# Retention attention and a PReLU block on one core: the first batch's two large parts in chunks of 128 tokens instead of 64, and three unread products ahead of the first unit instead of two

## The chip, the cores and the metric

The kernel runs on one core of one Trainium2 chip. The metric is the device time of one execution in microseconds, and lower is better. The time before is the median of 9 runs. A profile was taken of one more execution; every duration below comes from it.

## What is computed

The reference is a retention layer (attention without a softmax, with a decay for the distance between tokens) over 8 batches, 8 heads, 576 tokens and 64 columns a head, followed by a two-layer block over all 8 x 576 = 4608 tokens. All of it is in float32.

```
scores = (q @ k.T) / sqrt(64)                     # per batch and head, 576 x 576
gamma  = 1 - 2 ** (-5 - h)                        # h = 0..7
D      = gamma ** (i - j) if i >= j else 0
x      = (scores * D) @ v                         # to (4608 tokens, 512)
h      = x @ w_in                                 # 512 -> 2048
g      = max(h, 0) + alpha * min(h, 0)
out    = g @ w_out                                # 2048 -> 512
```

The decay splits into a factor for the query's place and one for the key's, so a sequence can be taken in chunks: inside a chunk the masked scores are multiplied by v; what earlier chunks give is a 64 x 64 state k.T @ v for each head, the running sum of the earlier chunks' products, multiplied by q.

## The kernel before

**Two phases on TensorE.** The two-layer block works on blocks of 256 tokens (`kb`, 18 of them) and on 8 slices of the 2048 columns (`i`). One pair (kb, i) is a unit. The units of blocks 0 and 1 are plain: `plain_unit` (line 419) makes 8 products of 128x128 by 128x256 into `ph` (L426), ACT makes the two halves of the activation (L430, L432), DVE joins them (L442), and `mlp_out`/`plain_out` (line 397) makes 4 products of 128x512 into `po` (L405). All later units go through a scheme of 7 products for 8 (L470, L388), for which GpSimd first combines the weights. The weights come in 32 pieces of 512 KB by DMA. Each piece is rewritten on its way: two ACT instructions (L296, L298, `piece_in`), three on DVE (L307, L310, L312) and one sum on GpSimd (L314, `piece_out`). Pieces 0 and 1 hold the first layer's weights of unit slice 0, pieces 2 and 3 the second layer's; pieces 4 to 7 do the same for slice 1, and so on.

**The first batch.** While the weights are on their way, the first batch's attention is done by functions of its own, and its token blocks are the plain ones. Its 576 tokens are cut into three parts (`PARTS`): two large ones of 256 tokens, x = 0 and x = 1, and a last one of 64. All eight heads of a part are done together, two heads to a pair (`c`, four pairs), one head on array rows or columns 0 to 63, the other on 64 to 127. For a large part these steps follow each other:

- `part_scale` (L675): GpSimd multiplies q and v by their factors.
- `part_transposes` (L695): TensorE turns k and q, ACT copies them to kT and qT (L702), DVE the last one of part 0 (L700).
- `part_scores` (L714): 32 products, each of one chunk of 64 tokens for one head, in four quarters of the array. In part 0 DVE multiplies by the mask (L721), in part 1 ACT copies (L723) and GpSimd multiplies (L724).
- `part_states` (L734): 32 products k.T @ v, one for each chunk of 64 and each head, then running sums over the four chunks: in part 0 by ACT copies and GpSimd sums (L742, L744), in part 1 by DVE (L746).
- `part_carry` (L750): GpSimd scales the last sum for the next part.
- `part_values`: 32 products of the masked scores with v (L762); then for each chunk that has a state before it (three in part 0, four in part 1) 16 products of 32 columns of the state with qT (L773), so 48 and 64. ACT copies the result into `xb` (L779, L781).

**The order.** Each engine takes its instructions in the order of the text at lines 823 to 890; there the parts' steps, the pieces and the first units are laid one after another by hand. After part 0's values TensorE makes two products of 128x512 that nothing reads (L842, "idle"), the transpose of alpha (L845), and the first plain unit (0, 0). Part 1's transposes stand around that unit's `mlp_out`, then come its scores and states, unit (0, 1), its values, the last part's transposes (L789), and the output products of (0, 1). The last part's scores are L798; later pairs of heads in the second phase go through L559, L577, L616 and L652.

**Buffers.** PSUM banks come from `ps_a` (two banks that rotate), `ps_h` and `ps_o` (by name: `pso0` to `pso3`). In part 0 kT, qT and the masked scores are tiles "g" of the pool `mlp`, which has three buffers in rotation; the units' own g tiles take the same three. In part 1 they lie in parts of `w_out` that are still unused.

A float32 product shows as two instructions on TensorE in the trace, each with its own weight load; a transpose shows as one. The lines around the unread products:

```
    idle = ps_h.tile([P, DM], FP32, tag="psh0", name="idle")
    for _ in range(2):
        nc.tensor.matmul(idle, ident, part[0][0][:, 0].rearrange("p h d -> p (h d)"),
                         start=True, stop=True)
```

Of the kernel before, what the change touches and what calls it, by code (L numbers as in the profile page):

```python
# [10 lines left out]
FP32 = mybir.dt.float32  # L11
# [7 lines left out]
def kernel(  # L19
# [121 lines left out]
    def room(i, s0, n):  # L141
# [5 lines left out]
        "p (m h d) -> p m h d", h=H, d=D) for i in (2, 3, 4)] for x in range(2)]  # L147
    part.append([room(i, 4, 2).rearrange("p (m h d) -> p m h d", h=H, d=D) for i in (2, 3, 4)])
    sums = [[room(i, s0, 1).rearrange("p (c d) -> p c d", d=D) for i, s0 in x] for x in (
        ((5, 4), (5, 5), (5, 6), (6, 4)), ((6, 5), (6, 6), (7, 4), (7, 5)), ())]  # L150
    carry = [None] + [room(i, 6, 1).rearrange("p (c d) -> p c d", d=D) for i in (2, 7)]

    def load_part(x):
# [26 lines left out]
    zero = const.tile([P, D], FP32, name="zero")  # L180
    nc.gpsimd.memset(zero, 0.0)

    mask = const.tile([P, C], FP32, name="mask")
    nc.gpsimd.memset(mask, 1.0)
    for p2 in range(2):
        nc.gpsimd.affine_select(out=mask[p2 * C:(p2 + 1) * C], in_=mask[p2 * C:(p2 + 1) * C],
                                compare_op=ALU.is_ge, fill=0.0, base=0, pattern=[[1, C]],
                                channel_multiplier=-1)

    dif = const.tile([P, NBIT, H], FP32, name="dif")  # L190
    for h in range(H):
# [358 lines left out]
    def pair_scores(n, kT, qT):  # L550
        c = pairs[n][1]

        mt = attn.tile([P, 2 * S], FP32, tag="at", name=f"mt_{n}").rearrange(
            "p (h j s) -> p h j s", h=2, s=C)
        ps = [ps_tile([P, NM, C], f"ps{p2}_{n}") for p2 in range(2)]
        for j in range(NJ):
            for h2 in range(2):
                x = (1 - h2, h2)[j % 2]
                nc.tensor.matmul(ps[j % 2][half(x), j // 2], kT[half(h2), chunk(j)],  # L559
                                 qT[half(h2), chunk(j)], start=True, stop=True)  # L560
        for h2 in range(2):
            nc.scalar.copy(mt[half(h2), h2].rearrange("p j s -> p (j s)"), qT[half(h2)])
        for p2 in range(2):
            for h2 in range(2):
                h, to, x = 2 * c + h2, half(1 - h2), (1 - h2, h2)[p2]
                nm = NM - p2
                nc.vector.scalar_tensor_tensor(
                    out=mt[to, h2, p2::2], in0=ps[p2][half(x), 0:nm], scalar=th[to, 3, h:h + 1],
                    in1=mask[to, None, :].to_broadcast([C, nm, C]), op0=ALU.mult, op1=ALU.mult)
        return mt  # L570

    def pair_states(n, kn, vn):
# [33 lines left out]
    def pair_front(n, kT, qT, kn, vn, extra):  # L606
# [20 lines left out]
        for h2 in range(2):  # L627
            to = half(1 - h2)
            nc.vector.scalar_tensor_tensor(  # L629
                out=mt[to, h2, NJ - 1], in0=extra[to],  # L630
                scalar=th[to, 3, 2 * c + h2:2 * c + h2 + 1], in1=mask[to],
                op0=ALU.mult, op1=ALU.mult)
        for p2 in range(2):
            for h2 in range(2):
                h, to, x = 2 * c + h2, half(1 - h2), (1 - h2, h2)[p2]
                nc.vector.scalar_tensor_tensor(  # L636
                    out=mt[to, h2, p2:NJ - 1:2], in0=ps[p2][half(x), 0],
                    scalar=th[to, 3, h:h + 1],
                    in1=mask[to, None, :].to_broadcast([C, NM - 1, C]),
                    op0=ALU.mult, op1=ALU.mult)  # L640
        later.append(lambda: pair_sums(vn, running_sums(n, ps[0][:, 1], ps[1][:, 1])))

# [44 lines left out]
    def part_transposes(x, i):  # L687
# [5 lines left out]
        for m in range(2):  # L693
# [7 lines left out]
            else:  # L701
                nc.scalar.copy(to, fro)  # L702

    def part_scores(x):
        at = tat[x] = (mlp.tile([P, 8 * P], FP32, tag="g", name=f"pa_{x}") if x == 0 else
                       room(4, 0, 4)).rearrange("p (h n) -> p h n", h=2)
        banks = part_banks(x, 2 if x == 0 else None, "ps")
        kT, qT = tT[x, 0], tT[x, 1]
        for m in range(2):
            for c in range(NPAIR):  # L710
                for p2 in range(2):
                    for h2 in range(2):
                        j = chunk(2 * m + p2)
                        nc.tensor.matmul(banks[h2][half(p2), (2 * c + m) * C:(2 * c + m + 1) * C],  # L714
                                         kT[half(h2), c, j], qT[half(h2), c, j],
                                         start=True, stop=True)
        for h2 in range(2):
            to, fro = [t.rearrange("p (n s) -> p n s", s=C) for t in (at[:, h2], banks[h2])]
            m = mask[:, None, :].to_broadcast([P, 8, C])
            if x == 0:  # L720
                nc.vector.tensor_tensor(out=to, in0=fro, in1=m, op=ALU.mult)  # L721
            else:
                nc.scalar.copy(to, fro)  # L723
                nc.gpsimd.tensor_tensor(out=to, in0=to, in1=m, op=ALU.mult)  # L724

    def part_states(x):
        kn, vn = part[x][0], part[x][2]
        banks = [t.rearrange("p (m c d) -> p m c d", m=2, c=NPAIR)
                 for t in part_banks(x, None if x == 0 else 0, "pu")]
        for m in range(2):  # L730
            for c in range(NPAIR):
                for p2 in range(2):
                    for h2 in range(2):
                        nc.tensor.matmul(banks[p2][half(h2), m, c], kn[half(p2), m, 2 * c + h2],  # L734
                                         vn[half(p2), m, 2 * c + h2],
                                         start=(m == 0 and c == 0),
                                         stop=(m == 1 and c == NPAIR - 1), skip_group_check=True)
        was = carry[x]
        for j in range(4):
            u = banks[j % 2][:, j // 2]  # L740
            if x == 0:
                nc.scalar.copy(sums[x][j], u)  # L742
                if j:
                    nc.gpsimd.tensor_tensor(out=sums[x][j], in0=was, in1=sums[x][j], op=ALU.add)  # L744
            else:
                nc.vector.tensor_tensor(out=sums[x][j], in0=was, in1=u, op=ALU.add)  # L746
            was = sums[x][j]

    def part_carry(x):
        nc.gpsimd.tensor_tensor(out=carry[x + 1], in0=sums[x][3],  # L750
                                in1=gch[:, 2, :, None].to_broadcast([P, NPAIR, D]), op=ALU.mult)

    def part_values(x):
        vn, qT, at = part[x][2], tT[x, 1], tat[x]
        banks = [t.rearrange("p (c m s) -> p c m s", c=NPAIR, m=2)
                 for t in part_banks(x, 0 if x == 0 else None, "pv")]
        for m in range(2):
            for c in range(NPAIR):
                for p2 in range(2):
                    for h2 in range(2):  # L760
                        n = 2 * c + m
                        nc.tensor.matmul(banks[p2][half(h2 ^ p2), c, m],  # L762
                                         vn[half(p2), m, 2 * c + h2],
                                         at[half(p2), h2, n * C:(n + 1) * C],
                                         start=(m == 0 and c == 0), stop=False,
                                         skip_group_check=True)
        for j in range(1 if x == 0 else 0, 4):
            su = sums[x][j - 1] if j else carry[x]
            for c in range(NPAIR):
                for h2 in range(2):  # L770
                    for e in range(0, D, 32):
                        to = (h2 ^ (j % 2)) * D + e
                        nc.tensor.matmul(banks[j % 2][to:to + 32, c, j // 2],  # L773
                                         su[half(h2), c, e:e + 32], qT[half(h2), c, chunk(j)],
                                         start=False, stop=(j >= 2), skip_group_check=True)
        xb[x] = ring.tile([P, NCC, TB], FP32, tag=f"x{x}", name=f"xb_{x}")
        to = xb[x].rearrange("p c (m q s) -> p q c m s", m=2, q=2)
        for c in (slice(0, 2), slice(2, 4)) if x == 0 else (slice(0, NPAIR),):
            nc.scalar.copy(to[:, 0, c], banks[0][:, c])  # L779
            for h2 in range(2):  # L780
                nc.scalar.copy(to[half(h2), 1, c], banks[1][half(1 - h2), c])  # L781


    def last_transposes():
# [8 lines left out]
    def last_scores():  # L793
# [5 lines left out]
                                 start=True, stop=True)  # L799
        for h2 in range(2):  # L800
            nc.vector.tensor_tensor(out=at[0:C, h2], in0=ps[h2][0:C],
                                    in1=mask[0:C, None, :].to_broadcast([C, NPAIR, C]),
                                    op=ALU.mult)

    def last_values():
# [23 lines left out]
    part_transposes(0, 0)  # L829
    part_transposes(0, 1)  # L830
    part_scale(0, 2)
    part_scores(0)
    piece_in(1)
    part_states(0)
    piece_in(2)
# [2 lines left out]
    part_values(0)  # L838

    idle = ps_h.tile([P, DM], FP32, tag="psh0", name="idle")  # L840
    for _ in range(2):
        nc.tensor.matmul(idle, ident, part[0][0][:, 0].rearrange("p h d -> p (h d)"),  # L842
                         start=True, stop=True)
    aps = ps_a.tile([P, NFC], FP32, tag="psa", name="aps")
# [13 lines left out]
    mlp_out(lambda: part_transposes(1, 1))  # L858
    piece_out(1)
    piece_in(1)  # L860
    part_scores(1)
    piece_out(1)
    part_states(1)
    piece_in(1)
# [167 lines left out]
```

## Time and profile before

| what | value |
|---|---|
| median of 9 runs | 1011.19 us (1009.38 to 1014.33) |
| the profiled execution | 1012.03 us, its span 1010.3 us |
| TensorE busy (PE) | 995.0 us, 98% of the span |
| VectorE busy (DVE) | 772.7 us, 76% |
| ScalarE busy (ACT) | 267.4 us, 26% |
| GpSimd busy (POOL) | 179.0 us, 18% |
| first product of L695, L714, L734, L762, L773 in part 0 | 5.15, 10.38, 12.14, 13.58, 14.92 us |
| first unread product (L842), first product of unit (0, 0) | 18.26, 20.40 us |
| first product of part 1's scores, of unit (0, 1), of part 1's values | 30.35, 34.58, 38.23 us |

The span runs from the first to the last recorded instruction of the core. PE is TensorE's products and PEld its weight loads, SP the engine that issues most DMAs. "L714" is line 714 of the kernel. In the chain that ended last, each piece shows its start, its duration and what ran, followed back from the last instruction through whatever released it; "issue" is time in which the profile shows nothing that the engine waited for. A window's row shows the window, its length, and for each engine the busy time and, in brackets, how many instructions were in flight in it, then the granted clock, the DMA share and GB/s. A share of busy time is a mean over the whole span; what a step in the first 50 us costs is read from windows and the timeline there.

### The profile page before, as it was taken

How to read it: one execution, taken by the hardware profiler on the slowest of the kernel's cores; microseconds unless marked ns; L12 is line 12 of the kernel's file. 1: busy time of each engine (PE TensorE's matmuls, PEld its weight loads, DVE VectorE, ACT ScalarE, POOL GpSimd, SP SyncE). 2: the span in 40 equal slices, each digit the busy share in tenths (PEclk: the TensorE clock that was granted, in tenths of full speed). 3: DMA queues.
4: the chain of work that ended last, by engine and by line, in shares of the span. 5: the costliest groups of instructions: out<-in, count | busy, mean ns of one | idle time of the engine just before them, and what ended most of it. 6: DMA issues, size and time to landing. Idle time of an engine off the chain costs nothing.

```text
span 1010.3 us, 23133 instructions
## 1 busy us (share of the span) xinstructions
PE 995.0 (98%) x9389; PEld 891.9 (88%) x9389; DVE 772.7 (76%) x2086; ACT 267.4 (26%) x605; POOL 179.0 (18%) x201
## 2 busy tenths in 40 slices
PE   6899999999999999999999999999999999999998
PEld 5666668999999999999999999999999999999997
DVE  7669967887878878686777788878778776666665
ACT  5556663222222222022122222222222210000000
POOL 5656674310100020100010000200010001010000
PEclk9999999999999999999999999999999999999999
DMA  9985745232322312131121122323222000000000
GB/s 229 245 201 140 185 73 120 49 72 48 69 48 49 68 37 63 18 69 31 40 48 48 36 56 48 69 48 69 48 43 52 13 22 1 22 1 22 1 22 22
DMA packets 229595, 64.30 MB, mean 64 GB/s; under 512 B 214368, under 2 KB 223088, under 8 KB 229488
## 3 DMA queue, kind: packets, MB, share of 16 engines
q1 hardware_dynamic: 227088, 62.02, 27.4%
q8 instruction: 74, 1.21, 0.5%
q10 hardware_dynamic: 2400, 0.79, 0.4%
q14 instruction: 33, 0.27, 0.1%
HBM read 53.35 MB, written 9.44 MB: 62 GB/s over the span
## 4 chain that ended last, share of the span: by engine, by line
PE 98%; DMA 1%; issue 0%; DVE 0%; ACT 0%; SPq 0%; DVEq 0%
PE ph L470 40%; PE po L388 38%; PE ph L426 6%; PE po L405 6%; PE pv L652 3%; PE ps L616 1%; PE ps L622 1%; DMA w_out<-in_k_dram 1%; PE pv L966 1%; PE pt L695 0%; PE ps L714 0%; PE ps L559 0%; PE pv L773 0%; PE pu L734 0%; PE pu L577 0%
## 5 line engine op out<-in xcount | busy, mean ns | idle before, releaser
L388 PE MATMUL po<-w_out,g 128*128 128x256 f32 x1792 | 408.2, 379 | 0.0
L388 PEld LDWEIGHTS po<-w_out,g 128*128 128x128 f32 x1792 | 330.7, 190 | 39.7
L481 DVE TENSOR_TENSOR g<-ph,g 128x256 f32<-128x256 f32 (+1 forms) x512 | 187.0, 386 | 135.3 <-PE ph L470 68.3
L470 PE MATMUL ph<-xb,w_in 128*128 128x128 f32 x2048 | 272.7, 276 | 0.0
L470 PEld LDWEIGHTS ph<-xb,w_in 128*128 128x128 f32 x2048 | 257.1, 192 | 7.4 <-issue 0.5
L470 PE MATMUL ph<-xt,w_in 128*128 128x128 f32 x1536 | 213.3, 275 | 0.0
L470 PEld LDWEIGHTS ph<-xt,w_in 128*128 128x128 f32 x1536 | 192.1, 192 | 0.0
L476 ACT COPY g<-ph 128x128 f32<-128x128 f32 x128 | 34.1, 266 | 403.9 <-PE ph L470 391.5
L492 DVE TENSOR_TENSOR g<-g 128x128 f32<-128x128 f32 x512 | 127.6, 290 | 7.0
L531 POOL TENSOR_TENSOR qx<-qx,tabx 128x576 f32<-128x576 f32 x28 | 32.7, 1170 | 354.4 <-DMA qx<-in_q_dram 174.1
L486 DVE SCALAR_TENSOR_TENSOR g<-g 128x512 f32<-128x512 f32 x128 | 89.8, 701 | 3.0
L484 DVE TENSOR_SCALAR g<-g,alpha 128x256 f32<-128x256 f32 x256 | 86.1, 378 | 3.7
L405 PE MATMUL po<-w_out,g 128*128 128x512 f32 x128 | 58.6, 599 | 0.9 <-DVE g L442 0.9
L426 PE MATMUL ph<-xb,w_in 128*128 128x256 f32 x256 | 58.6, 383 | 0.0
L663 ACT COPY xb<-pv 128x256 f32<-128x256 f32 (+3 forms) x84 | 23.2, 315 | 126.5 <-PE pv L652 126.5
L426 PEld LDWEIGHTS ph<-xb,w_in 128*128 128x128 f32 x256 | 47.9, 190 | 9.3 <-issue 2.4
L600 ACT COPY vn<-su 64x512 f32<-64x512 f32 x56 | 34.5, 616 | 78.9 <-DVE su L594 78.5
L636 DVE SCALAR_TENSOR_TENSOR mt<-ps,th,mask 64x256 f32<-64x256 f32 x96 | 46.4, 483 | 2.2
L456 POOL TENSOR_TENSOR xt<-xb 128x256 f32<-128x256 f32 x16 | 11.6, 726 | 195.2 <-PE ph L470 195.2
L405 PEld LDWEIGHTS po<-w_out,g 128*128 128x128 f32 x128 | 23.4, 190 | 24.5 <-issue 21.8
L629 DVE SCALAR_TENSOR_TENSOR mt<-pv,th,mask 64x64 f32<-64x64 f32 x48 | 13.6, 283 | 40.1 <-ACT xb L663 39.8
L536 ACT ACTIVATE vn<-vn,tabv 64x576 f32<-64x576 f32 x56 | 43.2, 772 | 1.6 <-DMA vn<-in_v_dram 0.4
(136 smaller groups left out, 738.1 us busy)
## 6 DMA issues: line engine op xcount, KB each, us to landing
out_dram<-osb SPq DMA_DIRECT2D x34, 256.0 KB, 2.1
kx<-in_k_dram SPq DMA_DIRECT2D x112, 72.0 KB, 2.7
qx<-in_q_dram SPq DMA_DIRECT2D x112, 72.0 KB, 3.0
vn<-in_v_dram SPq DMA_DIRECT2D x56, 144.0 KB, 3.3
kn<-in_k_dram SPq DMA_DIRECT2D x56, 144.0 KB, 3.7
raw<-in_moe_w_in_dram SPq DMA_DIRECT2D x24, 256.0 KB, 4.6
raw<-in_moe_w_out_dram SPq DMA_DIRECT2D x10, 512.0 KB, 4.5
w_in<-in_moe_w_out_dram SPq DMA_DIRECT2D x6, 512.0 KB, 6.2
```

Of the source, the lines that this page charges most:

```text
L388: nc.tensor.matmul(acc[kb][n // 2][:, n % 2, :], g[:, x, :], w_out[i][:, y, :], start=(i == 0 and n % 2 == 0), stop=(i == NU - 1 and (n % ...
L405: nc.tensor.matmul(acc[kb][m], g[:, 2 * x + m], w_out[i][:, 2 * x:2 * x + 2].rearrange("p x f -> p (x f)"), start=(i == 0 and x == 0), sto ...
L426: nc.tensor.matmul(ph[:, x], w_in[i // UST][:, cc // 2 * 2 + x, i % UST, cc % 2], xb[kb][:, cc], start=(cc == 0 and x == 0), stop=(cc == N ...
L470: nc.tensor.matmul(ph[m][:, o], w_in[i // UST][:, l, i % UST, cc], r[:, cc], start=(n in (0, 3) and cc == 0), stop=(n in (2, 6) and cc == ...
L476: nc.scalar.copy(g[:, 7], ph[0][:, 2])
L481: nc.vector.tensor_tensor(out=o, in0=x0, in1=x1, op=ALU.add)
L484: nc.vector.tensor_scalar(g[:, 4 + 2 * m:6 + 2 * m], g[:, 2 * m:2 * m + 2], 0.0, alpha[:, fc:fc + 1], ALU.min, ALU.mult)
L486: nc.vector.scalar_tensor_tensor(out=g[:, 0:4].rearrange("p x t -> p (x t)"), in0=g[:, 0:4].rearrange("p x t -> p (x t)"), scalar=0.0, in1 ...
L492: ins = nc.vector.tensor_tensor(out=g[:, o, :], in0=g[:, x0, :], in1=g[:, x1, :], op=op)
L536: nc.scalar.activation(vn[x, h2], vn[x, h2], ACTF.Copy, scale=tabv[x, c:c + 1])
L600: nc.scalar.copy(vn[half(h2), h2, 1:], su[half(h2)])
L636: nc.vector.scalar_tensor_tensor(out=mt[to, h2, p2:NJ - 1:2], in0=ps[p2][half(x), 0], scalar=th[to, 3, h:h + 1], in1=mask[to, None, :].to_ ...
```

## The change

Both large parts are taken in two chunks of 128 tokens (`m`) instead of four of 64.

- Scores: 16 products with 64 rows, 128 columns and 128 columns of data instead of 32 of 64x64 with 64. The masked tile doubles, to two tiles of 128 x 1024, one for each head of the pairs. In both parts head 0's (h2 = 0) two halves are multiplied by the mask on DVE, head 1's are copied by ACT and multiplied by GpSimd.
- The mask is one 128x128 triangle; the other users take a 64x64 corner of it.
- States: 16 products over 128 rows instead of 32 over 64, in one bank instead of two, and two sums instead of four.
- Values: 16 products of 128x64 with 128 columns of data, all eight for head 0 ahead of all eight for head 1; then 8 products (part 0) or 16 (part 1) of 64x64 state with 128 columns of qT instead of 48 and 64. The copies to `xb` are four in part 0 and two in part 1, all over 128 partitions.
- Part 1's head-1 scores take a "g" tile, and the PSUM banks of the steps are dealt out anew.
- Three unread products stand ahead of the first unit instead of two.

```diff
-    mask = const.tile([P, C], FP32, name="mask")
-    nc.gpsimd.memset(mask, 1.0)
-    for p2 in range(2):
-        nc.gpsimd.affine_select(out=mask[p2 * C:(p2 + 1) * C], in_=mask[p2 * C:(p2 + 1) * C],
...
+    mask2 = const.tile([P, P], FP32, name="mask2")
+    nc.gpsimd.memset(mask2, 1.0)
+    nc.gpsimd.affine_select(out=mask2, in_=mask2, compare_op=ALU.is_ge, fill=0.0, base=0,
+                            pattern=[[1, P]], channel_multiplier=-1)
...
     def part_scores(x):
+        at = tat[x] = [(mlp.tile([P, 8 * P], FP32, tag="g", name=f"pa{h2}_{x}") if x == 0 or h2
+                        else room(4, 0, 4)).rearrange("p (c s) -> p c s", c=NPAIR)
+                       for h2 in range(2)]
+        banks = part_banks(x, 2 if x == 0 else None, "ps0"), part_banks(
+            x, None if x == 0 else 0, "ps1")
         kT, qT = tT[x, 0], tT[x, 1]
         for m in range(2):
+            to = slice(m * P, (m + 1) * P)
             for c in range(NPAIR):
-                for p2 in range(2):
-                    for h2 in range(2):
-                        j = chunk(2 * m + p2)
-                        nc.tensor.matmul(banks[h2][half(p2), (2 * c + m) * C:(2 * c + m + 1) * C],
-                                         kT[half(h2), c, j], qT[half(h2), c, j],
-                                         start=True, stop=True)
+                for h2 in range(2):
+                    nc.tensor.matmul(banks[h2][m][:, c * P:(c + 1) * P], kT[half(h2), c, to],
+                                     qT[half(h2), c, to], start=True, stop=True)
+        return banks
+
+    def part_masks(x, banks, h2):
+        for m in range(2):
+            to = tat[x][h2][:, :, m * P:(m + 1) * P]
+            fro = banks[h2][m].rearrange("p (c s) -> p c s", c=NPAIR)
+            w = mask2[:, None, :].to_broadcast([P, NPAIR, P])
+            if h2 == 0:
+                nc.vector.tensor_tensor(out=to, in0=fro, in1=w, op=ALU.mult)
             else:
                 nc.scalar.copy(to, fro)
-                nc.gpsimd.tensor_tensor(out=to, in0=to, in1=m, op=ALU.mult)
+                nc.gpsimd.tensor_tensor(out=to, in0=to, in1=w, op=ALU.mult)
...
     def part_states(x):
...
+                for h2 in range(2):
+                    nc.tensor.matmul(u[half(h2), m, c], kn[:, m, 2 * c + h2],
+                                     vn[:, m, 2 * c + h2], start=(m == 0 and c == 0),
+                                     stop=(m == 1 and c == NPAIR - 1), skip_group_check=True)
         was = carry[x]
+        for m in range(2):
             if x == 0:
+                nc.scalar.copy(sums[x][m], u[:, m])
+                if m:
+                    nc.gpsimd.tensor_tensor(out=sums[x][m], in0=was, in1=sums[x][m], op=ALU.add)
             else:
+                nc.vector.tensor_tensor(out=sums[x][m], in0=was, in1=u[:, m], op=ALU.add)
+            was = sums[x][m]
...
     def part_values(x):
...
+        su = [carry[x], sums[x][0]]
+        for h2 in range(2):
+            for m in range(2):
+                for c in range(NPAIR):
+                    nc.tensor.matmul(banks[m][half(h2), c], vn[:, m, 2 * c + h2],
+                                     at[h2][:, c, m * P:(m + 1) * P], start=(c == 0),
+                                     stop=(su[m] is None and c == NPAIR - 1),
+                                     skip_group_check=True)
         for m in range(2):
...
             for c in range(NPAIR):
                 for h2 in range(2):
...
+                    nc.tensor.matmul(banks[m][half(h2), c], su[m][half(h2), c],
+                                     qT[half(h2), c, m * P:(m + 1) * P], start=False,
+                                     stop=(c == NPAIR - 1), skip_group_check=True)
         for c in (slice(0, 2), slice(2, 4)) if x == 0 else (slice(0, NPAIR),):
+            for m in range(2):
+                nc.scalar.copy(xb[x][:, c, m * P:(m + 1) * P], banks[m][:, c])
...
-    part_scores(0)
+    banks = part_scores(0)
+    part_masks(0, banks, 0)
+    part_masks(0, banks, 1)
...
-    for _ in range(2):
+    for _ in range(3):
         nc.tensor.matmul(idle, ident, part[0][0][:, 0].rearrange("p h d -> p (h d)"),
```

## The prediction

> **What bounds the kernel now.** I read the shares of busy time first, then the chain that ended last in order of time, then narrow windows of its first 46 us. The page:
>
> ```profile
> span 1010.3 us, 23133 instructions
> PE 995.0 (98%) x9389; PEld 891.9 (88%) x9389; DVE 772.7 (76%) x2086; ACT 267.4 (26%) x605; POOL 179.0 (18%) x201
> ...
> q8 instruction: 74, 1.21, 0.5%
> ...
> PE 98%; DMA 1%; issue 0%; DVE 0%; ACT 0%; SPq 0%; DVEq 0%
> ```
>
> TensorE is busy in all but 15.3 us, and the chain that sets the end lies on it for 98%. So a change in TensorE's first 46 us comes out at the end unless a wait there takes it up. The chain through that stretch (start, duration, what):
>
> ```profile
> 7.51 2.94 PE pt L695 x12
> 10.45 1.92 PE ps L714 x64
> 12.37 1.38 PE pu L734 x64
> 13.75 1.24 PE pv L762 x64
> 14.99 0.35 PE pv L773 x14
> 15.34 1.78 issue
> 17.13 1.21 PE pv L773 x77
> 18.33 1.91 PE idle L842 x4
> 20.25 0.16 PE aps L845
> 20.41 3.69 PE ph L426 x16
> ...
> 30.42 1.09 PE ps L714 x64
> 31.51 0.93 PE pu L734 x62
> 32.44 1.94 issue
> 34.38 0.27 PE pu L734 x2
> 34.65 3.65 PE ph L426 x16
> 38.30 1.09 PE pv L762 x64
> 39.39 1.34 PE pv L773 x89
> ```
>
> The reader is to see the four steps of each part (scores L714, states L734, values L762 and L773), two products that nobody reads (L842), and two holes called "issue", 1.78 and 1.94 us, in the middle of a group where nothing is waited for. I take the holes for TensorE waiting for its own code. The queue q8 brought 74 packets in 1.21 MB, one per 254 of TensorE's 18,778 instructions. Before the first hole TensorE had run 222 products with 222 weight loads, 444 instructions; between the holes lie 253 with their loads, 506, about two packets. In the DMA view one q8 packet falls in 14.5 to 17 us and one in 30.5 to 33.5. The packet missing at 32.44 was due about 254 instructions after 30.3 us and came at 34.38: some 4 us, against the 2.1 in which those instructions were used up. A packet's worth used more slowly than in 4.5 us shows no hole.
>
> **The change, the first part.** All times are starts of instructions in the timeline; one product is two instructions.
>
> *Scores.* 32 products of 64x64 on quarters of the array become 16 of 64 rows and 128 columns over 128 columns of data. In L714 four quarters run at once, and a set of four 64-column instructions starts every 0.107 us until about 13.2 us and every 0.058 after (the first L714 group averages 314 ns, the second 221): the array's clock doubles there, though the granted clock reads 1.00 throughout. 128 columns thus cost 0.213 and then 0.113 (L470, 128 columns: 40% of 1010.3 us over 3,584 instructions, 0.113). Two row halves do run side by side: L798 is made of such pairs and its 16 instructions take 0.52 us. So 16 pairs: 13 at 0.213 and 3 at 0.113, 3.1 us from 10.38, against 1.76 from L714's start to L734's. **+1.4**; scores end at 13.5.
>
> *States.* 16 products of 128 rows on column halves. L652 has this shape and starts a pair every 0.058: 16 pairs, 0.93, and 0.1 for the changed tiling (L762 to L773: 0.15 between starts instead of 0.06). Before 1.44. **-0.4**; they end at 14.6.
>
> *Values.* The masks double (four 128x512 instead of two) and head 1's go over ACT and POOL. Its buffer is the one kT lies in, so ACT's copy waits until all scores are done: 13.9. Two copies at 0.58 (L723), then two POOL products at 1.28 (L724): 14.5 to 15.8 and to 17.1. The last four products, eight instructions at 0.113, end at 18.0. The carried part is now 8 products instead of 48, in pairs: 0.1 + 8 x 0.113 = 1.0, to 19.0. Before 18.26. So the hole goes, and a wait for POOL's second mask stands in its place: without that wait the values would end near 17.4. **First part in all +0.8.**
>
> *The third unread product.* L842's instructions start 0.43 apart: **+0.86**, on the path. The first unit starts 1.7 later than 20.40, at 22.1.
>
> *What else is late by then.* ACT's conversion of the first weight piece (L296 at 11.98, behind the copies now) starts at 15.1, and DVE's (L307) at 15.8 instead of 13.70. POOL, which now does two masks and one sum for three sums, ends pieces 0 and 1 at about 19.3 and 21.4; the first unit needs them at 22.1 and 23.8. The four copies to xb (0.37 each, no half copies any more) run from 19.9 to 21.4, under the unread products. These covers are 0.7 us and more. The smaller mask constants (two GpSimd instructions instead of three, at 1.7 us) lie in POOL's idle time.
>
> **The second part**, all at the full clock. Scores 16 pairs at 0.113 plus start, 1.84 against 0.92: **+0.9**. States 1.05 against 3.31 (31.27 to 34.58, hole included): **-2.3**. They need the bank of the first DVE mask, free at 33.9 by my times, as the scores end: no wait. Instruction 444 is now reached here, since the first part now issues 256 instructions (transposes included) instead of 608, and 254 of them nowhere pass in under 4.5 us: both holes go. Carried part: 16 pairs at 0.113 and two changes of tiling, 2.05, against 2.07 from L773's start to L789's: **0**; the wait of L789 for ACT's copies (0.3) goes with it.
>
> *Values, second part: the cost I can only bound.* 16 products of 128 columns, the first eight on one column half, the last eight on the other. One after the other: 32 x 0.113 = 3.6. If TensorE starts the second half's while the first half's queue: 1.8. L773 decides between them. It has 16 products on four tiles and then 16 on four others; with four at work, equal windows must show equal counts:
>
> ```profile
> 39.41:39.59 0.18, 0.18 (x20) 0.18 (x23) 1.00 1.15 455
> 39.59:39.77 0.18, 0.18 (x37) 0.18 (x27) 1.00 0.88 364
> ```
>
> 20 instructions are in flight in the first window and 37 in the second: the later tiles' have started while 12 of the first 32 had not. The window is deep enough for eight products. I take 1.85 against 1.09: **+0.75**, and keep 3.6. POOL's masks are done by 37.2, the values start at 38.6.
>
> Second part: 0.9 - 2.3 + 0.75 + 0 = **-0.6**. Sum: 0.8 + 0.86 - 0.6 = **+1.1 us**. Weights for later units stand ready 8 us ahead (POOL ends unit 2's second piece at 50.6, TensorE takes it near 60), so nothing takes the 1.1 up. The profiled execution took 1012.03 (span 1010.3 and 1.7 around it), 0.8 above the median of nine: 1013.1 by its own time, **1012.3** by the median 1011.19.
>
> Two rules of the Trainium skill speak against this sum. "TensorE: Matmul & The Clock Gate", Part 3, has matmuls start strictly in program order; the two windows above disagree, and by the rule the values would cost 3.6 and the sum would be +2.9. "Runtime: NRT & Kernel Launch", Instruction fetch mechanics, calls the cost of crossing a 16 KiB block of code mostly hidden; here 1.78 and 1.94 us stand bare. By that rule the holes have another cause and may stay, and the sum would be +3.0 to +4.8.
>
> **The rivals.** (1) *The column halves run one after the other* in the second part: 3.6 instead of 1.85, +1.8, sum +2.9, 1014.1, slower. It decides as soon as fewer than eight products may be overtaken; against it stand the 20 and 37, for it that those are tiles of 32 columns and these are whole column halves. The first part hardly notices, as POOL's mask is late there anyway. (2) *The holes stay or come elsewhere*: the change doesn't save code where it matters. One hole of 1.9 in the second part gives 1014.2, a further one 1016. For it: the DMA engines are over 90% busy there. Against it: the packet counts fit to within 5%. (3) *The first part costs nothing*: if POOL's masks or the row pairs are quicker than their rows, or the first unit starts as early as now, only the second part's -0.6 and some tenths are left, 1010 to 1010.6. No row gives more, so faster by over 0.2% needs something I don't see, such as the array's clock rising earlier for wider products (at 10.4 instead of 13.2: -1.3 at most).
>
> **How the numbers follow.** A difference within 0.2% (2.0 us) is about what a measurement of this kernel can't tell from none. Forecast 0.45 (1010.8 to 1013.8); column halves 0.15; holes 0.15; first part free 0.10; something unseen 0.15, half of it faster. Slower by over 0.2% means above 1013.2: rivals 1 and 2, the forecast's upper end and part of the unseen, 0.40. Within 0.45. Faster, below 1009.2, 0.15. The range from 1009.4 takes in rival 3, and to 1015.4 rivals 1 and 2 with one hole.
>
> **What the profile after would show.** Right: no "issue" piece over 0.5 us before 40 us; L842's successor x6 and 2.6 us; values of the first part ending on POOL near 19 us; the first ph group at 22.1; in the second part values of some 1.85 us and states next to scores without a hole; the second part's transposes near 42.5 instead of 41.4. Wrong: a values group of 3.6 us at 38.6 (rival 1), a hole inside a group (rival 2), the first ph group before 21 us (rival 3), or a row-half pair taking 0.226 instead of 0.113, which would add some 4 us.

## The result, and the profile after

The changed kernel takes **1013.98 us**, the median of 9 runs (1013.66 to 1014.71). The 29 runs of the kernel before that stand beside them have a median of 1011.10 (1009.12 to 1014.33). The ratio is 1.0029, with a 95% interval of 1.0020 to 1.0038: slower by 0.29%. The forecast was 1012.3, the range 1009.4 to 1015.4; the time lies in the range, next to the first rival's 1014.1.

Its profiled execution took 1013.53 us. First the page of the kernel after: the span, the busy times of the engines (share, instructions), the code queue q8 (packets, MB, share), and the chain's shares by engine.

```profile
span 1011.8 us, 22397 instructions
PE 1000.6 (99%) x9023; PEld 896.6 (89%) x9023; DVE 773.3 (76%) x2086; ACT 266.1 (26%) x602; POOL 180.0 (18%) x200
...
q8 instruction: 71, 1.16, 0.5%
...
PE 98%; DMA 1%; POOL 0%; DVE 0%; ACT 0%; issue 0%; SPq 0%; DVEq 0%; POOLq 0%; ACTq 0%
```

TensorE has 366 instructions for products fewer (9389 to 9023), q8 brings three packets of code fewer, and yet TensorE is busy 5.6 us longer. That is the first thing to read here: the small tiles that went had been running four at a time, so fewer instructions were not less time, and the holes that went were not busy time. POOL has come into the chain ahead of DVE, and "issue" has gone down in it.

Then the chain of the kernel after through the first 45 us (start, duration, what):

```profile
7.23 2.97 PE pt L698 x12
10.20 2.39 PE ps L719 x32
...
12.67 0.60 ACT pa L731
...
13.40 2.52 POOL pa L732 x2
...
15.96 1.09 PE pv L772 x8
17.05 1.02 PE pv L781 x16
18.07 2.77 PE idle L849 x6
...
21.00 3.70 PE ph L429 x16
...
31.02 1.99 PE ps L719 x32
...
33.05 1.15 PE pu L746 x32
34.20 3.65 PE ph L429 x16
37.85 3.26 PE pv L772 x32
```

The two holes are gone: no "issue" piece in this stretch is over 0.2 us. In the first part the chain leaves TensorE at the end of the scores, goes over ACT's first copy (L731) and POOL's two masks (L732), and comes back for the last eight values instructions, as forecast. The six instructions of the unread products take 2.77. The part that doesn't fit is the last line: part 1's values take 3.26 us where 1.85 was forecast.

By starts, the difference of the two profiled executions is made of these terms:

| step | before | after | difference | forecast |
|---|---|---|---|---|
| part 0, from scores to the first unread product | 7.88 | 7.87 | 0 | +0.8 |
| unread products | 1.92 | 2.77 | +0.85 | +0.86 |
| part 1, scores | 0.98 | 2.10 | +1.12 | +0.9 |
| part 1, states with the hole | 3.25 | 1.08 | -2.17 | -2.3 |
| part 1, values | 1.09 | 3.26 | +2.17 | +0.75 |
| part 1, carried part | 2.07 | 1.89 | -0.18 | 0 |
| the chain's first transposes end earlier | 10.38 | 10.13 | -0.25 | none |

The sum is 1.54, and the spans differ by 1.5. The prediction's 0.92 and 3.31 count the states from their first weight load, at 31.27; the table counts products, from 31.33. The medians differ by 2.9: the execution of before in the profile was 0.9 above its kernel's median of 29, and the one of after 0.45 below its own.

How part 1's values run is seen in TensorE's timeline of the kernel after. Here w_out holds head 0's masked scores and pa head 1's, and each head has 16 instructions on its own column half:

```profile
37.78 1.63 PE L772 MATMUL pv<-w_out,w_out 128*64 128x128 f32 x13
39.15 0.32 PE L772 MATMUL pv<-pa,w_out 128*64 128x128 f32 x1
39.25 0.27 PE L772 MATMUL pv<-w_out,w_out 128*64 128x128 f32 x1
...
39.52 1.58 PE L772 MATMUL pv<-pa,w_out 128*64 128x128 f32 x13
```

Thirteen of head 0's instructions start before the first of head 1's, the last three alternate with it, and then thirteen of head 1's stand alone. So a free column half did start ahead of queued work of the other one, but only past three instructions, not past sixteen.

### The profile page after: what moved, and what is told of

It is laid out like the page before. It is cut to its first block, busy times and chain, and to the rows that moved or that the text cites. A ratio compares the mean times of both kernels' runs of the same rounds, so it can differ in the third digit from the quotient of the medians.

```text
span 1011.8 us, 22397 instructions
## 1 busy us (share of the span) xinstructions
PE 1000.6 (99%) x9023; PEld 896.6 (89%) x9023; DVE 773.3 (76%) x2086; ACT 266.1 (26%) x602; POOL 180.0 (18%) x200
## 4 chain that ended last, share of the span: by engine, by line
PE 98%; DMA 1%; POOL 0%; DVE 0%; ACT 0%; issue 0%; SPq 0%; DVEq 0%; POOLq 0%; ACTq 0%
PE ph L473 40%; PE po L391 38%; PE ph L429 6%; PE po L408 6%; PE pv L655 3%; PE ps L619 1%; PE ps L625 1%; DMA w_out<-in_k_dram 1%; PE pv L975 1%; PE ps L719 0%; PE pv L772 0%; PE pt L698 0%; PE ps L562 0%; PE pv L781 0%; PE idle L849 0%; POOL pa L732 0%
## 5 line engine op out<-in xcount | busy, mean ns | idle before, releaser
L534 POOL TENSOR_TENSOR qx<-qx,tabx 128x576 f32<-128x576 f32 x28 | 32.9, 1175 | 352.9 <-DMA qx<-in_q_dram 253.6
```

## The experiments

**Which order makes part 1's values cheap.** The changed kernel, with part 1's values taking the heads in turn:

```diff
-        for h2 in range(2):
-            for m in range(2):
-                for c in range(NPAIR):
+        for h2, m, c in ([(h2, m, c) for h2 in range(2) for m in range(2) for c in range(NPAIR)]
+                         if x == 0 else
+                         [(h2, m, c) for m in range(2) for c in range(NPAIR) for h2 in range(2)]):
```

> The changed kernel, but in the second part the 16 value products take the two heads in turn (m, c, head) instead of all eight of head 0 first. Theory (look-ahead of a few products only, so the column halves run one after the other): the second part's values group shrinks from 3.26 us to about 1.85, and the time falls by 1.4 us from 1013.98 to 1012.6. Rival (the group is slow for its masks, its bank or its 128 columns, not for the order): 3.2 us again and 1014.0.

Measured: 1012.56 (1011.94 to 1013.47), 1.42 below the changed kernel; ratio to before 1.0014 (1.0004 to 1.0024). The changed kernel was not run again beside this one, and the kernel before had a median of 1010.71 here and 1011.10 there. Counted from the runs of before beside each, the order is worth 2.88 - 1.85 = 1.03. The chain's piece:

```profile
38.36 1.90 PE pv L772 x32
```

1.90 instead of 3.26, by the order of the same 16 products. Each head's instruction now starts within 0.01 us of the other's, every 0.11 us.

**How far TensorE looks ahead.** The same, but in runs of four products of one head (`for m`, `for h2`, `for c`), in part 1 only.

> The changed kernel, but the second part's values go by chunk, then head: runs of four products on a column half instead of eight. Theory (TensorE looks ahead past about four instructions of the same half, so a run's last four go beside the next run's first four): 20 starts of 0.11 instead of 28, the values group 2.4 us instead of 3.26, the time 1013.1. Rival A (the overlap of four seen at the switch is a matter of chance or of the mask's semaphore): 3.3 us, 1014.0. Rival B (runs of four are already within the window): 1.9 us as with heads in turn, 1012.6.

Measured: 1013.19 (1012.48 to 1013.67), ratio 1.0027 (1.0017 to 1.0037). In the chain, and then in the timeline where the values start:

```profile
38.04 2.50 PE pv L772 x32
...
37.97 0.76 PE L772 MATMUL pv<-w_out,w_out 128*64 128x128 f32 x5
38.46 0.32 PE L772 MATMUL pv<-pa,w_out 128*64 128x128 f32 x1
38.56 0.27 PE L772 MATMUL pv<-w_out,w_out 128*64 128x128 f32 x1
```

2.50 lies between 1.90 and 3.26, where the theory of a short look-ahead put it. The timeline shows the same depth: five of head 0's first run of eight instructions start, then head 1's first starts ahead of the remaining three. With runs of one product the halves run side by side all the way, with runs of eight hardly at all.

The Trainium skill, "TensorE: Matmul & The Clock Gate", Part 3, has matmuls begin and end strictly in program order. By the start times of the changed kernel and of the run in fours they do not: up to three instructions of a busy column half are passed. (With the heads in turn the starts keep the program's order.) The rule's 3.6 us is nearer to the 3.26 measured than the 1.85 forecast was.

**The third unread product alone.** The changed kernel with two of them:

```diff
-    for _ in range(3):
+    for _ in range(2):
```

> The changed kernel with two unread products instead of three. Theory (they lie on the path, and nothing else is late): the first unit starts 0.86 us earlier, at 20.1 us, and the time falls by 0.86 to 1013.1. Rival (something else sets the first unit, or the array's clock falls without the third): 1014.0 or more, with a hole before the first unit or instructions at half the rate behind it.

Measured: 1012.99 (1012.35 to 1013.66), 0.99 below the changed kernel; ratio 1.0020 (1.0010 to 1.0030). Counted from the runs of before beside each, it is 2.88 - 2.28 = 0.60. From the chain:

```profile
18.70 1.91 PE idle L849 x4
...
37.62 3.26 PE pv L772 x32
```

The unread products take 1.91 instead of 2.77, and the values stay at 3.26. The trace's 0.86 lies between the two differences of medians: the product's price comes out at the end, to within some 0.3 us.

**The third unread product in the kernel before.**

> The kernel before with three unread products instead of two, and nothing else. Theory: +0.86 us, 1011.1 to 1012.0, the first unit at 21.3 us. Rival (a product more gives the code or the weights time that is saved later, in the hole at 32.4 us): within 0.3 us of before.

Measured: 1011.31 (1009.76 to 1015.94) against 1010.71 of the kernel before beside it; ratio 1.0006 (0.9992 to 1.0020). The interval holds the theory's end and the rival's, so this run does not decide. Its profile says why it is a poor place to measure: the second hole is gone from part 1's states (L734 takes 0.93), a short one of 0.43 between starts stands in part 1's values instead, the first hole has grown to 2.12, and right after it the unread products run at half the rate. From the chain of this kernel:

```profile
14.65 2.12 issue
16.77 1.28 PE pv L773 x77
18.05 4.34 PE idle L842 x6
```

Six instructions at 0.43 would be 2.6. In the windows (window, length, the engines' busy times, then the granted clock, the DMA share and GB/s) the clock falls at that place:

```profile
18.20:21.60 3.40, 3.40 (x5) 1.48 (x6) 1.39 (x2) 3.32 (x8) 2.48 (x3) 0.56 0.94 239
```

**What the holes are.** The kernel before, with 24 small products that nothing reads ahead of the first transposes (96 instructions with their loads), while TensorE waits for k anyway:

```diff
+    ahead = [ps_h.tile([P, DM], FP32, tag=f"psh{i}", name=f"ahead{i}") for i in range(2)]
+    for n in range(6):
+        for p2 in range(2):
+            for h2 in range(2):
+                nc.tensor.matmul(ahead[h2][half(p2), n * C:(n + 1) * C],
+                                 ident[half(h2), 0:C], ident[half(h2), 0:C],
+                                 start=True, stop=True, skip_group_check=True)
     part_transposes(0, 0)
```

> The kernel before with 24 products of 64x64 of the identity with itself (96 instructions of TensorE, results unread) put ahead of the first transposes, where TensorE waits for the first DMA until 5.15 us. Theory (the two holes are TensorE waiting for its own code, at fixed places in its instruction stream): the first hole moves 96 instructions forward in the program, from the carried part (L773) into the values L762, some 15 products in, still 1 to 2 us long; the second, which was in the states of the second part, would fall at the border of its scores and states and is half as long or gone. Rival (the holes are waits for data of these products): both stay at the same products, the 14th instruction of L773 and the last pair of L734, with the lengths of before. The array's clock may double earlier, which would take up to 1 us off the time.

Measured: 1016.39 (1013.19 to 1021.21), ratio 1.0053 (1.0034 to 1.0073). The chain of this kernel:

```profile
13.37 0.68 PE pv L762 x29
14.05 0.70 issue
...
16.79 3.61 issue
...
35.49 0.23 PE pu L734 x15
35.72 0.56 issue
...
43.61 2.04 issue
```

The holes moved with the count of instructions. Counted in TensorE's whole stream, with the records of its waits for semaphores (which the prediction's 444 left out), this kernel's four stalls stand after 449, 705, 961 and 1473 instructions (the fourth is in part 1's values). In the kernel before, they stand after 449 and 961; with three unread products in it, after 449 and, the short one, 1217. All the distances are whole multiples of 256. The products on which they fall are others, so a wait for the data of certain products is refuted. The DMA records have one packet of q8, 16 KB and 1.0 to 1.4 us long, that starts 2.2 to 2.9 us ahead of the end of each hole of this kernel and of the kernel before. What the prediction said of the pace, that a packet's worth used more slowly than in 4.5 us shows no hole, fell with the stall at 961: the block before it had been entered at 20.40, 15 us earlier, and the packet still came only near 33.5. When TensorE asks for a block stays open. Not forecast: the holes after 705 and 1473, and a fall of the granted clock to 0.50 from 20.6 to 24.0 us:

```profile
20.60:24.00 3.40, 3.40 (x5) 1.15 (x4) 0.00 (x0) 3.23 (x8) 0.69 (x1) 0.50 1.01 215
```

"Runtime: NRT & Kernel Launch", Instruction fetch mechanics, in the Trainium skill has code come in blocks of 256 instructions, and the trace agrees with that step. It also has the cost of crossing a block mostly hidden. Here four crossings of the first 46 us cost 0.56 to 3.61 us.

**A version without the three costs.** The changed kernel, with the values' heads in turn in both parts, all four masks of part 0 on DVE (each half of the tokens for both heads, then the next), and two unread products:

```diff
-            if h2 == 0:
+            if h2 == 0 or x == 0:
...
-    part_masks(0, banks, 0)
-    part_masks(0, banks, 1)
+    for m in range(2):
+        for h2 in range(2):
+            part_masks(0, banks, h2, (m,))
...
-    for _ in range(3):
+    for _ in range(2):
```

> The changed kernel with the values of both parts taking the heads in turn, all four masks of the first part on DVE (first chunk's two, then the second's) instead of two over ACT and GpSimd, and two unread products. Theory: the masks are done 1.1 us earlier than GpSimd's, so the first part ends 1.1 us earlier and no longer waits for GpSimd; with 1.4 for the second part's order and 0.86 for the product, 1013.98 becomes 1010.6. Rival (the first part's end is then set by something else, DVE's own masks or the first weight piece, which DVE now reaches no earlier): the first unit starts no earlier than with the masks on GpSimd, 1011.7.

Measured: 1010.68 (1010.23 to 1011.64) against 1010.64 of the kernel before beside it; ratio 1.0000 (0.9991 to 1.0009). So the change's loss of 2.9 is found, to within the interval's 0.9 us. In its chain the first part stays on TensorE, and POOL comes in later, with the scaling of part 1's q (L678):

```profile
13.85 2.07 PE pv L772 x32
...
16.94 1.91 PE idle L850 x4
...
26.12 1.01 POOL w_out L678
```

From the scores' end to the unread products' start it takes 4.17 us instead of 5.48. Some of that is handed back at once: from the first output products to part 1's scores it takes 5.00 us here and 4.48 in the run with two unread products, since the transposes now wait for POOL.

**With one unread product, and with none.** The same version with `range(1)`, and with the unread products left out.

> The kernel with heads in turn and all first masks on DVE, with one unread product. Theory: another 0.86 us off, 1009.8, the first unit at about 18.1 us after the scores of a fast start. Rival (the array's clock falls to half behind the short wait that now stands there): a stretch at clock 0.5 of some 3.4 us and up to 1.7 us lost, 1011 to 1012.

> The kernel with heads in turn and all first masks on DVE, with no unread product at all. Theory: the first unit now waits for its first weight piece (GpSimd, about 18.3 us) and the copies to xb instead of for TensorE, so no more than 0.2 us is won over one unread product, 1009.6. Rival 1 (the clock falls in the wait of about 1.5 us): a stretch at clock 0.5, up to 1.7 us lost, 1011. Rival 2 (nothing but TensorE stood in the way): 1008.9.

Measured: 1010.75 (1009.99 to 1011.50), ratio 0.9998 (0.9990 to 1.0007) with one; 1010.80 (1010.01 to 1012.32), ratio 0.9999 (0.9989 to 1.0010) with none. Both expectations fell: nothing was gained. With one, the first unit starts 1.3 earlier than with two (17.71 against 19.00), but the second part's transposes end within 0.1 of the same time (27.72 and 27.83). The chain goes back through DMAs instead:

```profile
20.56 4.11 DMA w_out<-in_q_dram
...
24.74 1.04 POOL w_out L678
```

With none, the first unit itself waits 1.15 us for POOL's sum of piece 0 (L317). So in this version the step from two unread products to one or none gains nothing that the medians show: the weights, k and q are late enough to hide it. With three in the changed kernel the product was on the path, as the run with two shows.

**Asking for q earlier.** One unread product, part 1's k, q and v asked for one weight piece earlier, and POOL's scaling of q ahead of its fourth sum:

```diff
-    fetch(6)
+    fetch(5)
     load_part(1)
...
+    part_scale(1, 1)
     piece_in(2)
     piece_out(1)
-    part_scale(1, 1)
     plain_unit(0, 0)
```

> The second part's k, q and v are asked for one piece of weights earlier, and q's scaling by POOL stands ahead of the fourth piece's last addition; one unread product, and masks and values as in the run with one unread product before it. Theory: that run gained nothing because the work behind the first unit waited for arrivals and not for TensorE: piece 1 (POOL) held the unit by 0.3 us, k and q held the transposes by 0.87, 0.41 and 0.33. With k and q earlier, the first half of the output products still can't start before the activations of the first unit (DVE's second L445 ended at 24.0 and the products began at 24.4), so those of 24.4 stay, the transposes of q follow at 26.1 and 26.7 in place of 26.1 and 27.06, and the gain is 0.3 to 0.4 us: 1010.3, within 0.2% of the kernel before. Rival: TensorE's own work was the limit, and the saved product was lost in noise; then the waits go and the gain is the whole product, 0.9 us, 1009.8.

Measured: 1011.57 (1010.43 to 1012.38), with 1011.79 for the kernel before beside it; ratio 1.0000 (0.9991 to 1.0008). The waits for k and q are gone (q's transposes run from 26.92 without a break), so the first step of the theory held. The forecast gain of 0.3 to 0.4 is not seen; the interval of 0.9 us to either side could not show it. A new wait shows in the timeline (the bracket is the idle time before and what ended it):

```profile
31.02 2.06 PE L719 MATMUL ps<-w_out,w_out 64*128 64x128 f32 x32 [1.35 <-ACT w_out L705]
```

ACT's copy of the turned q stands behind its conversion of a later weight piece (L299). That piece was now asked for after q and landed at 29.18; ACT had waited 3.82 us for it. In the run with one unread product the same conversion started at 25.09. So here q came earlier and this piece some 4 us later, in a stretch (16 to 32 us) whose windows of 4 us have a DMA share of 0.80 to 1.10. No version here is shown to beat the kernel before.

## Where the prediction was right, and where it was off

- **The direction and the first-rank steps.** The path lies on TensorE, so what is added there comes out: confirmed by the term table (sum 1.54, spans 1.5) and by the unread product (0.85 in the trace, 0.60 to 0.99 between medians). The sum's +1.1 was 1.8 short of the medians' +2.9; the time lies in the range because the range took in rival 1's price. The likeliest class, a difference within 0.2%, had 0.45 and did not come; slower by more had 0.40 and came.
- **The failed step** is part 1's values, "The window is deep enough for eight products. I take 1.85 against 1.09: +0.75". It measured +2.17. The two windows of L773 showed that 12 instructions of the first 32 were overtaken, and I read that as a depth in instructions altogether. But those 12 lay on four tiles, three on each. The three passed in the changed kernel, and in the run in fours, are the same depth on one tile: all of them fit a depth that is counted for each tile of the array, and none fits one for the whole queue. The mechanism of rival 1 (fewer than eight may be overtaken) decided, with 3.26 instead of its 3.6. Taking the heads in turn gave 1.90, which shows that the price of a pair behind the 1.85 was right and the order was what failed.
- **Part 1's scores**: +1.12 for +0.9. The pairs take 0.11 each, as forecast, but the first takes 0.21, and 0.32 pass from the last pair (32.73) to the first product of the states (33.05). The prediction saw no wait there. The states need the bank that DVE's first mask reads, and DVE's two masks (L729) run for 1.51 from 32.21, so the first ends near 32.9; how much of the 0.32 is that wait, no run separates.
- **The holes**: both went, with the terms -2.17 for -2.3 and the first one's 1.78. That they are TensorE waiting for its own code was argued in the prediction; the shifted kernel shows that they go by the count of instructions.
- **Part 0**: +0.8 was forecast and 0 stands in the table. The mechanism is right: from the scores' end to the part's end it took 5.48, 5.48, 5.48 and 5.49 us in the changed kernel and in the runs with heads in turn, two unread products and runs of four, always through ACT's copy and POOL's two masks. What differs is the scores: 2.39 us in the changed kernel's profile, 3.03, 3.13 and 2.81 in the other three, where 3.1 was forecast. The array's doubling to full rate, put at 13.2 us, came near 10.9 in that one profile. From the scores' start to the unread products it took 8.51, 8.61 and 8.30 in those three, +0.4 to +0.7 on before's 7.88. So +0.8 was somewhat high, and the 0 is one execution's luck; in the profiles it hid 0.8 of the 1.4 that part 1's values cost over their forecast.
- **From profile to median.** The forecast took the profiled execution of before 0.8 above its median and carried the difference over. That understated the loss: the medians differ by 2.9, the profiles by 1.5. Between medians the costs are 1.42 for the values' order, 0.99 for the third product and, from there to the version with DVE's masks, 1013.98 - 1.42 - 0.99 - 1010.68 = 0.89 for part 0, 3.3 in all. Counted from the runs of before beside each, they are 1.03, 0.60 and 2.88 - 1.03 - 0.60 - 0.04 = 1.21, 2.8 in all. The traces have 1.36, 0.86 and 5.48 - 4.17 - 0.52 = 0.79, 3.0. So the three together are about what was lost, and each is known to some 0.4 us. That the holes' gain went to the longer scores and values is read from the table; no run of its own shows it.

## What to carry to other kernels

Products that can run side by side on different parts of the array should stand next to each other in the program: a loop that does all of one half and then all of the other took 3.26 us where the same products in turn took 1.90. When a trace shows work being overtaken, count how many instructions are passed on each tile before using that as a depth. Here fewer, larger products saved the code's arrival but not TensorE's time, since the small tiles had already run four at once; and after a step is off the path, look for the transfer behind it before promising its time.

## What the runs showed of the hardware that was not expected

- **A hole can cost twice.** After a hole of 2.12 us (three unread products in the kernel before) and after one of 3.61 (shifted kernel) the unread products ran at half rate for some 3.4 us, 1.6 and 1.7 us lost (4.34 for 2.77, 3.59 for 1.91). After the 1.78 and 1.94 of the first profile, and after the shifted kernel's 2.04, nothing fell. The Trainium skill, "TensorE: Matmul & The Clock Gate", Part 1, gives an idle window of about 3.4 us ahead of the lower clock; one of 2.12 was enough here.
- **That goes with the scatter of the kernel before.** Of its 79 runs that stand beside the experiments, 24 list a mean clock of 0.998, with a median of 1012.34; the other 55 list 0.999 or 1.0, with 1010.32. The changed kernel, which has no holes, lists 1.0 in all ten runs, the profiled one with them, and scatters over 1.2 us; the 29 runs of before beside it scatter over 5.2. That the low-clock runs are those with a longer hole fits the profiles of the two kernels above; none of the kernel before's own low-clock runs was profiled.
- **The array's start-up.** By the steps between the starts of products, the first instructions at full rate came at 13.1 us before, 10.9 after, and 12.2 and 12.4 in the runs with heads in turn and with two unread products, while the granted clock read 1.00 in these windows. What sets the moment stays open.
